# Decayed block attention followed by an ELU MLP: chunk 3 handled by head halves in separate PSUM banks, with the masks and the state work placed elsewhere

## The chip, the cores and the metric

The kernel runs on one core of one Trainium2 chip. The metric is the device time of one execution in microseconds (us), the median of several runs. A core has TensorE (PE in the profile; its weight loads are PEld), VectorE (DVE), ScalarE (ACT), GpSimd (POOL), and SyncE (SP), which here only issues transfers. Transfers issued by POOL go through one software queue (q0), those of SP and ACT through hardware queues; all share the core's 16 DMA engines.

## The reference

```python
# q, k, v: (4, 8, 768, 64) float32; lam: 8 decays near 0.98; w_in: 512 x 2048; w_out: 2048 x 512
block, nb = 64, S // 64
rel = pos[:, None] - pos[None, :]
Dmask = np.where(rel >= 0, lam[:, None, None] ** rel[None], 0.0)
lam_pow = lam[:, None, None] ** (pos[None, :, None] + 1)
lam_block = lam ** block
for b in range(nb):
    intra = np.einsum('bhic,bhjc->bhij', qb, kb) * Dmask[None]
    intra = np.einsum('bhij,bhjd->bhid', intra, vb)
    inter = np.einsum('bhid,bhde->bhie', qb * lam_pow[None], kv_state)
    out[:, :, sl] = intra + inter
    rev_pow = lam[:, None, None] ** (block - 1 - pos[None, :, None])
    kv_state = lam_block[None, :, None, None] * kv_state + np.einsum('bhsd,bhse->bhde', kb * rev_pow[None], vb)
# then, with x = out as (3072, 512):
h = x @ w_in
g = np.where(h > 0.0, h, np.exp(np.minimum(h, 0.0)) - 1.0)
return (g @ w_out).astype(np.float32)
```

## The kernel before, in words

The sequence is cut into blocks of L = 128 positions, not 64. A *chunk* g is one such block of one batch item: g = 4*(block) + (batch item), 24 chunks in all, so chunks 0 to 3 are the first block of the four items and have no incoming state. Four chunks make a token tile t of 512 rows, and there are six tiles. The input arrives as float32 and is cast to float16 by the transfer.

For a chunk, `att_T` transposes q and k on TensorE (L217) and `att_Te` copies the result out of PSUM to qT and kT (L229); `att_S` forms the scores (psS, L263); `att_mask` multiplies them by the decay mask on VectorE, giving P (L275); `att_O` multiplies P by v (L289) and, from the second block on, adds q times the state (L297); `att_X` writes the result to xt, the input of the MLP (L316, L318 for chunks 0 to 3, and L320 with the factor qs for later ones). `att_kd` scales k (L250), `att_U` forms the state's increment (psU, L337), `att_tmp` scales the old state on POOL (tmp, L354), and `att_st` makes the new state (L371 for the first block, a copy; L373 later, an addition). The state tiles `st` are zeroed first by memsets (L114), since only their diagonal head blocks are written. From chunk 10 on, q and k are transposed in pairs by transfers issued on SP (`att_xT`, L238).

For a tile, `mm1` computes one of 16 slices n of h (four matmuls into psH, L390), ScalarE makes e = exp(h) (L416) and r = relu(h) (L420), and VectorE combines them to g (L433). For three slices of tile 0 (`alt`) ScalarE makes e only, and VectorE does the rest in two operations (L428, L431). `mm2` adds slice n of one chunk to its output psM (L471); after n = 15 the output is copied (L485, L487) and stored (L488). The very last chunk is done by `mm2_last` in two halves of 256 columns (L446, L456, L458, L459).

The order is written by hand; each engine executes its instructions in program order. A head part treats chunks 0 to 3 one by one, with `warm(k)` fillers (matmuls on a constant, L497; their counts are the list W). Then come the steps A0 to A15 (mm1 of tile 0, from A10 on also mm2 of chunks 0 and 1), B0 to B15 (mm2 of chunks 2, 0 and 1), the steps (1, 0) to (5, 15), and E. At a step, mm1 comes first, then what `at` has put there, then the combination to g, then mm2. `visit(g, s0, s1, s2)` puts the parts of a pair of chunks at three steps: transposes and kd, scores and mask, output and state.

Inputs are loaded by POOL in the order of LOADS: q, k, v of chunks 0 to 3, w_in in seven pieces (wi), w_out in four (wo), and the later chunks in pairs. kd of chunks 0 and 2 stands in that list too and runs on POOL. LOADS 17 to 26 (up to the last wo) are issued before step A0, the rest at later steps.

PSUM has four kinds of buffers, each with two: S (two banks each), M and H (one bank each). A buffer is handed on when its readers have finished. The mask of the first block (`mask`, built for even and odd heads by `build_mask0`) is overwritten at A1 by `late_mask` with the mask of the later blocks.

Of the kernel before, what the change touches and what calls it, by code (L numbers as in the profile page):

```python
# [15 lines left out]
def kernel(  # L16
# [96 lines left out]
    def zero_state(j, i):  # L113
        nc.vector.memset(st[j][i][:], 0.0)  # L114

# [25 lines left out]
    lag = cpool.tile([128, 128], FP32, name="lag")  # L141
    nc.vector.tensor_copy(rel[:], rel_i[:])
    nc.vector.tensor_scalar_max(lag[:], rel[:], 0.0)
# [11 lines left out]
    )  # L155

# [11 lines left out]
    dn = cpool.tile([128, H], FP32, name="dn")  # L168
    nc.scalar.activation(dn[:], loglam[:], AF.Exp, scale=pos[:, 0:1])
# [5 lines left out]
    def late_mask():  # L175
        for hh in range(2):
            nc.vector.tensor_tensor(
                out=mask[:, hh],
                in0=causT[:].unsqueeze(1).broadcast_to([128, HP, 128]),
                in1=dn[:, hh::2].unsqueeze(2).broadcast_to([128, HP, 128]),  # L180
                op=ALU.mult,
            )

    def late_qs():
        nc.scalar.activation(ks[:], loglam[:], AF.Exp, scale=pos[:, 1:2])
        for hh in range(2):
            r = slice(hh * 64, (hh + 1) * 64)
            nc.scalar.copy(loglam_p[r, :], loglam[r, hh::2])
        nc.scalar.activation(up_p[:], loglam_p[:], AF.Exp, scale=float(L))
        for hp in range(HP):  # L190
            nc.scalar.activation(
                qs[:, hp, :], row[:], AF.Exp, scale=loglam_p[:, hp : hp + 1]
            )
# [28 lines left out]
    def att_Te(g, n, which, eng):  # L222
        j = "qk".index(which)
        pt = pT.pop((g, j))
        dst = asb.tile([128, n, HP, 128], FP16, tag=f"{which}T", name=f"{which}T{g}", bufs=3)
        if eng == "v":
            nc.vector.tensor_copy(dst[:], pt)
        else:
            nc.scalar.copy(out=dst[:], in_=pt)  # L229
        for i in range(n):  # L230
            (qT, kT)[j][g + i] = dst[:, i]

# [36 lines left out]
    def att_mask(g, parts=1):  # L269
        P = asb.tile([128, 2, HP, 128], FP16, tag="P", name=f"P{g}", bufs=3)  # L270
        s = pS.pop(g)
        w = HP // parts
        for i in range(parts):
            c = slice(i * w, (i + 1) * w)
            nc.vector.tensor_tensor(  # L275
                out=P[:, :, c], in0=s[:, :, c],
                in1=mask[:, :, c], op=ALU.mult,
            )
        Pt[g] = P
# [25 lines left out]
    def att_X(g, n, parts=1):  # L305
        t, i = where[g]
        if i == 0:
            xt[t] = asb.tile([128, HP, TS[t] * L], FP16, tag="xt", name=f"xt{t}")
        po = pS.pop(("O", g))
        w = HP // parts  # L310
        for j in range(parts):
            c = slice(j * w, (j + 1) * w)
            dst = xt[t][:, c, i * L : (i + n) * L].rearrange("p h (n l) -> p n h l", n=n)
            if g < B:
                if j == 1:
                    nc.vector.tensor_copy(dst, po[:, :, c])  # L316
                else:
                    nc.scalar.copy(out=dst, in_=po[:, :, c])  # L318
                continue
            nc.vector.tensor_tensor(  # L320
                out=dst, in0=po[:, :, c],
                in1=qs[:, c].unsqueeze(1).broadcast_to([128, n, w, 128]),
                op=ALU.mult,
            )
# [36 lines left out]
    def att_st(g):  # L361
        c, b = divmod(g, B)
        if c == NC - 1:
            return
        pu = pS.pop(("U", g))
        new = st[b // 2][(c + 1) % 2]
        for hh in range(2):
            r = slice(hh * 64, (hh + 1) * 64)
            if c == 0:
                copy = nc.scalar.copy if g in (0, 2) else nc.vector.tensor_copy  # L370
                copy(out=new[r, :, :, r], in_=pu[r])  # L371
            else:
                nc.vector.tensor_tensor(  # L373
                    out=new[r, :, :, r], in0=tmps[g][r], in1=pu[r], op=ALU.add
                )
        tmps.pop(g, None)
# [18 lines left out]
    def mm1(t, n, alt=False):  # L395
# [15 lines left out]
        else:  # L411
            if (t, n) not in pH_of:
                mm1_mm(t, n, 0, MT, "M" if t == 0 and n % 2 == 1 and n < 8 else "H")
# [23 lines left out]
    def mm2_last(t, i):  # L437
# [3 lines left out]
        hw = DM // 2  # L441
        for x in range(2):
            pm = ps.tile([128, hw], FP32, tag="M", bufs=2, name=f"psM{t}_{i}_{x}")
            cs = slice(x * hw, (x + 1) * hw)
            for n in range(NF):
                nc.tensor.matmul(  # L446
                    pm[:], lhsT=gt[t][:, n, i * L : (i + 1) * L],
                    rhs=wo_t[wo_at[n][0]][:, wo_at[n][1], cs],
                    start=(n == 0), stop=(n == NF - 1),
                )  # L450
            parts = 1 if x == 0 else 2
            w = hw // parts
            for y in range(parts):
                o = msb.tile([128, w], FP32, tag="osb", bufs=3, name=f"osl{x}{y}")
                if y == 0:
                    nc.vector.tensor_copy(o[:], pm[:, 0:w])  # L456
                else:
                    nc.scalar.copy(o[:], pm[:, w:])  # L458
                (nc.sync if y == 0 else nc.scalar).dma_start(  # L459
                    out=out[t0 : t0 + L, x * hw + y * w : x * hw + (y + 1) * w], in_=o[:]  # L460
                )
# [29 lines left out]
    def warm(k):  # L491
        if k <= 0:
            return
        pw = ps.tile([128, 4, 128], FP32, tag="M", bufs=2, name=f"psW{len(warms)}")
# [24 lines left out]
    W = [5, 2, 3, 0, 1, 0, 0, 0, 0, 0, 0]  # L519
# [7 lines left out]
    late_qs()  # L527
# [14 lines left out]
    zero_state(0, 1)  # L542
# [10 lines left out]
    att_O(1, 1, "M")  # L553
    warm(W[8])
    op_T(3, "k")
    op_Te(3, "k")
    att_X(1, 1)
# [4 lines left out]
    warm(W[9])  # L562
    for n in range(0):
        mm1_mm(0, n, 0, 3 * L, "HM"[n % 2])
    att_O(3, 1, "M")
    att_X(3, 1, 2)
    zero_state(1, 1)
    warm(W[10])
    for n in range(0, 1):
        mm1_mm(0, n, 0, 3 * L, "HM"[n % 2])  # L570
    for n in range(1):
        mm1_mm(0, n, 3 * L, 4 * L)

    at(('A', 1), late_mask)
    at(('A', 4), zero_state, 0, 0)
    at(('A', 4), zero_state, 1, 0)
    run_loads(LOADS[17:27])
    for s, g in zip([], (0, 2)):
        at(s, att_kd, g, 2)
    for s, g in zip([('A', 7), ('A', 9)], (0, 2)):  # L580
        at(s, att_U, g)
    for s, g in zip([('A', 8), ('A', 10)], (0, 2)):
        at(s, att_st, g)
        at(s, att_tmp, g + B)
# [25 lines left out]
    for g, vs in [(4, (('A', 12), ('A', 14), ('B', 1))), (6, (('B', 7), ('B', 10), ('B', 13))), (8, ((1, 0), (1, 2), (1, 5))), (10, ((1, 8), (1, 10), (1, 13))), (12, ((2, 0), (2, 2), (2, 5))), (14, ((2, 8), (2, 10), (2, 13))), (16, ((3, 0), (3, 2), (3, 5))), (18, ((3, 8), (3, 10), (3, 13))), (20, ((4, 0), (4, 2), (4, 5))), (22, ((4, 8), (4, 10), (4, 13)))]:  # L610
        visit(g, *vs)
    for s, a, b in [(('A', 14), 27, 28), (('A', 15), 28, 29), (('B', 11), 29, 30), (('B', 13), 30, 31), ((1, 1), 31, 32), ((1, 5), 32, 33), ((1, 9), 33, 34), ((1, 13), 34, 35)]:
# [3 lines left out]
    for s, m1, m2 in steps:  # L616
        er = None
        if m1 is not None:
            t, n = m1
            er = mm1(t, n, alt=t == 0 and n in (3, 5, 7))  # L620
# [36 lines left out]
```

## Time and profile before

| | us |
|---|---|
| median of 7 runs (lowest to highest) | 218.83 (218.29 to 220.65) |
| the profiled execution | 218.79 |
| its span, first to last instruction | 217.0 |
| PE busy in the span | 202.9 (94%) |
| DVE / ACT / POOL busy | 148.1 / 129.0 / 78.8 |
| PE busy in 40.00:45.00 | 3.57 of 5 |
| PE busy in 60.00:65.00 and in 75.00:90.00 | 5.00 of 5 and 15.00 of 15 |

The span is what the profile's views cover; 1.8 us lie around it. A busy PE only says that matmuls are in flight, so the place to look is where PE is idle and what ended that idle time. The mean granted TensorE clock is 1.000. A timeline row gives the start, the duration, the engine, the line, the operation, output<-input, the shape and the number of merged instructions; the brackets give the idle time before it on its engine and what ended it.

### The profile page before, as it was taken

How to read it: one execution, taken by the hardware profiler on the slowest of the kernel's cores; microseconds unless marked ns; L12 is line 12 of the kernel's file. 1: busy time of each engine (PE TensorE's matmuls, PEld its weight loads, DVE VectorE, ACT ScalarE, POOL GpSimd, SP SyncE). 2: the span in 40 equal slices, each digit the busy share in tenths (PEclk: the TensorE clock that was granted, in tenths of full speed). 3: DMA queues.
4: the chain of work that ended last, by engine and by line, in shares of the span. 5: the costliest groups of instructions: out<-in, count | busy, mean ns of one | idle time of the engine just before them, and what ended most of it. 6: DMA issues, size and time to landing. Idle time of an engine off the chain costs nothing.

```text
span 217.0 us, 3963 instructions
## 1 busy us (share of the span) xinstructions
PE 202.9 (94%) x1583; PEld 100.3 (46%) x1583; DVE 148.1 (68%) x190; ACT 129.0 (59%) x244; POOL 78.8 (36%) x76
## 2 busy tenths in 40 slices
PE   5867889799999999999999999999999999999992
PEld 1343335455554544544544545445445444444461
DVE  2466997978799999989886785775665544434010
ACT  6966799331978676466566466466556666674110
POOL 8999959998732947680400000000000000000000
PEclk9999999999999999999999999999999999999999
DMA  5999999999999999999952061061011011110221
GB/s 38 147 154 176 207 168 181 178 183 157 183 203 133 158 155 174 158 178 184 147 124 73 3 136 61 0 145 52 0 50 51 0 48 50 48 51 0 97 96 51
DMA packets 98899, 23.86 MB, mean 110 GB/s; under 512 B 90944, under 2 KB 95936, under 8 KB 98880
## 3 DMA queue, kind: packets, MB, share of 16 engines
q0 software_dynamic: 80208, 13.63, 82.3%
q1 hardware_dynamic: 18528, 9.90, 20.3%
q8 instruction: 12, 0.20, 0.4%
q10 hardware_dynamic: 144, 0.07, 0.1%
q14 instruction: 7, 0.06, 0.1%
HBM read 27.27 MB, written 6.29 MB: 155 GB/s over the span
## 4 chain that ended last, share of the span: by engine, by line
PE 68%; DMA 14%; POOL 8%; DVE 5%; ACT 2%; issue 1%; POOLq 0%; ACTq 0%
PE psM L471 32%; PE psH L390 28%; DMA kn<-in_k_dram 7%; DMA kT<-kn 5%; POOL tmp L354 3%; POOL qn L72 2%; DMA qn<-in_q_dram 2%; PE psS L263 2%; PE psO L289 2%; DVE g L433 2%; POOL kn L72 2%; PE psM L446 2%; PE psO L297 1%; POOL vn L72 1%; ACT r L420 1%
## 5 line engine op out<-in xcount | busy, mean ns | idle before, releaser
L390 PE MATMUL psH<-xt,wi 128*128 128x512 f16 (+2 forms) x388 | 97.7, 377 | 1.4 <-DVE g L431 0.7
L471 PE MATMUL psM<-wo,g 128*128 128x512 f16 x368 | 94.3, 380 | 0.6 <-DMA wo<-in_moe_w_out_dram 0.5
L433 DVE SCALAR_TENSOR_TENSOR g<-e,r 128x512 f16<-128x512 f32 x93 | 70.5, 776 | 35.5 <-ACT r L420 35.3
L416 ACT ACTIVATE e<-psH 128x512 f32<-128x512 f32 x96 | 57.5, 600 | 56.2 <-PE psH L390 52.6
L390 PEld LDWEIGHTS <-wi 128*128 128x128 f16 x388 | 37.5, 98 | 46.5 <-issue 2.5
L420 ACT ACTIVATE r<-psH 128x512 f16<-128x512 f32 x93 | 55.4, 596 | 0.0
L471 PEld LDWEIGHTS <-g 128*128 128x128 f16 x368 | 34.6, 98 | 41.0 <-DMA wo<-in_moe_w_out_dram 1.0
L275 DVE TENSOR_TENSOR P<-psS,mask 128x1024 f16<-128x1024 f32 (+1 forms) x28 | 28.7, 1066 | 5.1 <-PE psS L263 5.1
L354 POOL TENSOR_TENSOR tmp<-st,up_p 64x512 f32<-64x512 f16 x16 | 21.2, 1325 | 9.0 <-DVE st L373 7.9
L72 POOL DMA_DIRECT2D vn<-in_v_dram x14 | 15.1, 1088 | 8.1 <-issue 8.1
L72 POOL DMA_DIRECT2D kn<-in_k_dram x14 | 15.2, 1087 | 6.0 <-issue 5.9
L72 POOL DMA_DIRECT2D qn<-in_q_dram x14 | 15.7, 1119 | 3.4 <-issue 3.4
L320 DVE TENSOR_TENSOR xt<-psO,qs 128x1024 f16<-128x1024 f32 x10 | 12.2, 1220 | 5.6 <-PE psO L297 5.6
L487 ACT COPY osb<-psM 128x512 f32<-128x512 f32 x12 | 7.0, 591 | 15.2 <-PE psM L471 15.2
L289 PE MATMUL psO<-P,vn 128*64 128x128 f16 x192 | 12.5, 223 | 2.3 <-DVE P L275 2.3
L289 PEld LDWEIGHTS <-vn 128*64 128x64 f16 x192 | 10.0, 109 | 7.4 <-issue 6.6
L485 DVE COPY osb<-psM 128x512 f32<-128x512 f32 x11 | 7.6, 689 | 5.5 <-PE psM L471 5.4
L250 DVE TENSOR_TENSOR kd<-kn,ks 128x1024 f16<-128x1024 f16 x8 | 11.2, 1400 | 0.1
L373 DVE TENSOR_TENSOR st<-tmp,psU 64x512 f16<-64x512 f32 x16 | 10.9, 681 | 0.2
L297 PE MATMUL psO<-qT,st 128*64 128x128 f16 x160 | 10.2, 219 | 0.0
L263 PE MATMUL psS<-qT,kT 64*128 64x128 f16 x192 | 8.0, 221 | 1.2 <-ACT kT L229 0.8
L297 PEld LDWEIGHTS <-st 128*64 128x64 f16 x160 | 9.0, 110 | 0.0
(51 smaller groups left out, 87.4 us busy)
## 6 DMA issues: line engine op xcount, KB each, us to landing
out_dram<-osb SPq DMA_DIRECT2D x23, 256.0 KB, 2.0
qn<-in_q_dram POOLq DMA_DIRECT2D x10, 256.0 KB, 15.7
kn<-in_k_dram POOLq DMA_DIRECT2D x10, 256.0 KB, 16.2
vn<-in_v_dram POOLq DMA_DIRECT2D x10, 256.0 KB, 16.6
wo<-in_moe_w_out_dram POOLq DMA_DIRECT2D x4, 512.0 KB, 13.7
wi<-in_moe_w_in_dram POOLq DMA_DIRECT2D x2, 512.0 KB, 9.5
wi<-in_moe_w_in_dram POOLq DMA_DIRECT2D x3, 256.0 KB, 7.2
qn<-in_q_dram POOLq DMA_DIRECT2D x4, 128.0 KB, 4.8
```

Of the source, the lines that this page charges most:

```text
L72: nc.gpsimd.dma_start(out=dst, in_=src[b : b + n, :, rows].rearrange("b h p d -> p (b h) d"))
L263: nc.tensor.matmul(s[:, hh, hp, :], lhsT=kT[g][r, hp, :], rhs=qT[g][r, hp, :], start=True, stop=True,)
L275: nc.vector.tensor_tensor(out=P[:, :, c], in0=s[:, :, c], in1=mask[:, :, c], op=ALU.mult,)
L289: nc.tensor.matmul(po[r, i, hp, :], lhsT=v_of(g + i, 2 * hp + hh), rhs=P[:, hh, hp, :], start=True, stop=(c == 0), skip_group_check=True,)
L297: nc.tensor.matmul(po[r, i, hp, :], lhsT=st[(g + i) % B // 2][c % 2][:, (g + i) % 2, hp, r], rhs=qT[g + i][:, hp, :], start=False, stop=Tr ...
L320: nc.vector.tensor_tensor(out=dst, in0=po[:, :, c], in1=qs[:, c].unsqueeze(1).broadcast_to([128, n, w, 128]), op=ALU.mult,)
L354: e.tensor_tensor(out=tmp[r], in0=old[r, :, :, r], in1=up_p[r].unsqueeze(1).unsqueeze(3).broadcast_to([64, 2, HP, 64]), op=ALU.mult,)
L390: nc.tensor.matmul(pH[:, lo:hi], lhsT=wi[:, kk, j * 128 : (j + 1) * 128], rhs=xt[t][:, kk, lo:hi], start=(kk == 0), stop=(kk == HP - 1),)
L416: nc.scalar.activation(e[:], pH[:], AF.Exp)
L420: nc.scalar.activation(r[:], pH[:], AF.Relu)
L433: nc.vector.scalar_tensor_tensor(out=g, in0=e[:], scalar=-1.0, in1=r[:], op0=ALU.add, op1=ALU.min)
L471: nc.tensor.matmul(pm[:], lhsT=gt[t][:, n, i * L : (i + 1) * L], rhs=wo_t[wo_at[n][0]][:, wo_at[n][1], :], start=(n == 0), stop=(n == NF - 1),
```

## The change

- The states' four memsets and both masks are made near the start, before `build_mask0`; the mask of the later blocks has a tile of its own, `mask1`. `lag` now shares the tile of `rel`.
- `late_qs` is split: ks, loglam_p and up_p stay (`late_up`), and the four rows of qs follow in two pairs, behind X(2) and behind the first mm1.
- X(0) is copied by VectorE. X(1) comes before the transposes of k(3).
- k(3)'s transposes and its copies (`att_T2`), and O(3) with X(3) (`att_OX2`), go by halves of the heads, each half in an H bank of its own; ScalarE copies the first half and VectorE the second.
- W has three more fillers: one each at W[5], W[8] and W[9].
- The slices of tile 0 below n = 8 use M for even n and H for odd n (it was the other way round), and `alt` applies to n = 2, 4, 6 instead of 3, 5, 7.
- `att_U` of chunks 0 and 2 moves from A7 and A9 to A5 and A7; `att_st` and `att_tmp` of them from A8 and A10 to A6 and A8. The state copy of chunk pair 0 goes to VectorE.
- The last two wo loads (LOADS 25 and 26) move from before A0 to A9 and A10.
- The third step of `visit(4)` (output and state) moves from B1 to B2.
- The last chunk is done in pieces of 256, 128 and 128 columns, in banks M, M and H, copied by VectorE, ScalarE and VectorE and stored from SP, ACT and SP.

```diff
     ]
-    def zero_state(j, i):
-        nc.vector.memset(st[j][i][:], 0.0)
-
...
     def run_loads(items):
...
     rel = cpool.tile([128, 128], FP32, name="rel")
-    lag = cpool.tile([128, 128], FP32, name="lag")
     nc.vector.tensor_copy(rel[:], rel_i[:])
-    nc.vector.tensor_scalar_max(lag[:], rel[:], 0.0)
     nc.vector.tensor_scalar(
...
     )
+    lag = rel
+    nc.vector.tensor_scalar_max(lag[:], rel[:], 0.0)
+    for j in range(B // 2):
+        for i in range(2):
+            nc.vector.memset(st[j][i][:], 0.0)
+    dn = cpool.tile([128, H], FP32, name="dn")
+    nc.scalar.activation(dn[:], loglam[:], AF.Exp, scale=pos[:, 0:1])
+    mask1 = cpool.tile([128, 2, HP, 128], FP32, name="mask1")
+    for hh in range(2):
+        nc.vector.tensor_tensor(
+            out=mask1[:, hh],
+            in0=causT[:].unsqueeze(1).broadcast_to([128, HP, 128]),
+            in1=dn[:, hh::2].unsqueeze(2).broadcast_to([128, HP, 128]),
+            op=ALU.mult,
+        )
     def build_mask0(hh):
...
     build_mask0(0)
-    dn = cpool.tile([128, H], FP32, name="dn")
-    nc.scalar.activation(dn[:], loglam[:], AF.Exp, scale=pos[:, 0:1])
     ks = cpool.tile([128, H], FP32, name="ks")
...
     loglam_p = cpool.tile([128, HP], FP32, name="loglam_p")
-    def late_mask():
-        for hh in range(2):
-            nc.vector.tensor_tensor(
-                out=mask[:, hh],
-                in0=causT[:].unsqueeze(1).broadcast_to([128, HP, 128]),
-                in1=dn[:, hh::2].unsqueeze(2).broadcast_to([128, HP, 128]),
-                op=ALU.mult,
-            )
-
-    def late_qs():
+    def late_up():
         nc.scalar.activation(ks[:], loglam[:], AF.Exp, scale=pos[:, 1:2])
...
         nc.scalar.activation(up_p[:], loglam_p[:], AF.Exp, scale=float(L))
-        for hp in range(HP):
+    def late_qs(lo, hi):
+        for hp in range(lo, hi):
             nc.scalar.activation(
...
             (qT, kT)[j][g + i] = dst[:, i]
+    def att_T2(g, which, tag):
+        j = "qk".index(which)
+        nat = heads((qn, kn)[j], g)
+        dst = asb.tile([128, 1, HP, 128], FP16, tag=f"{which}T", name=f"{which}T{g}", bufs=3)
+        w = HP // 2
+        for x in range(2):
+            t1 = ps.tile([128, w, 128], FP16, tag=tag, bufs=2, name=f"psT{which}{g}_{x}")
+            for y in range(w):
+                hp = x * w + y
+                nc.tensor.transpose(
+                    t1[:, y, :], in_=nat[:, 2 * hp : 2 * hp + 2, :], identity=ident16[:]
+                )
+            copy = nc.vector.tensor_copy if x else nc.scalar.copy
+            copy(out=dst[:, 0, x * w : (x + 1) * w], in_=t1[:])
+        (qT, kT)[j][g] = dst[:, 0]
+    def att_OX2(g, tag):
+        t, i = where[g]
+        P = Pt.pop(g)
+        w = HP // 2
+        for x in range(2):
+            po = ps.tile([128, w, 128], FP32, tag=tag, bufs=2, name=f"psO{g}_{x}")
+            for y in range(w):
+                hp = x * w + y
+                for hh in range(2):
+                    r = slice(hh * 64, (hh + 1) * 64)
+                    nc.tensor.matmul(
+                        po[r, y, :], lhsT=v_of(g, 2 * hp + hh), rhs=P[:, hh, hp, :],
+                        start=True, stop=True, skip_group_check=True,
+                    )
+            copy = nc.vector.tensor_copy if x else nc.scalar.copy
+            copy(out=xt[t][:, x * w : (x + 1) * w, i * L : (i + 1) * L], in_=po[:])
     def att_xT(g):
...
                 out=P[:, :, c], in0=s[:, :, c],
-                in1=mask[:, :, c], op=ALU.mult,
+                in1=(mask if g < B else mask1)[:, :, c], op=ALU.mult,
             )
...
             if g < B:
-                if j == 1:
-                    nc.vector.tensor_copy(dst, po[:, :, c])
-                else:
-                    nc.scalar.copy(out=dst, in_=po[:, :, c])
+                copy = nc.vector.tensor_copy if g == 0 else nc.scalar.copy
+                copy(out=dst, in_=po[:, :, c])
                 continue
...
             if c == 0:
-                copy = nc.scalar.copy if g in (0, 2) else nc.vector.tensor_copy
+                copy = nc.scalar.copy if g in (2,) else nc.vector.tensor_copy
                 copy(out=new[r, :, :, r], in_=pu[r])
...
             if (t, n) not in pH_of:
-                mm1_mm(t, n, 0, MT, "M" if t == 0 and n % 2 == 1 and n < 8 else "H")
+                mm1_mm(t, n, 0, MT, "M" if t == 0 and n % 2 == 0 and n < 8 else "H")
             pH = pH_of.pop((t, n))
...
         t0 = b * S + c * L
-        hw = DM // 2
-        for x in range(2):
-            pm = ps.tile([128, hw], FP32, tag="M", bufs=2, name=f"psM{t}_{i}_{x}")
-            cs = slice(x * hw, (x + 1) * hw)
+        x0 = 0
+        for x, (w, tag) in enumerate([(256, 'M'), (128, 'M'), (128, 'H')]):
+            pm = ps.tile([128, w], FP32, tag=tag, bufs=2, name=f"psM{t}_{i}_{x}")
             for n in range(NF):
...
                     pm[:], lhsT=gt[t][:, n, i * L : (i + 1) * L],
-                    rhs=wo_t[wo_at[n][0]][:, wo_at[n][1], cs],
+                    rhs=wo_t[wo_at[n][0]][:, wo_at[n][1], x0 : x0 + w],
                     start=(n == 0), stop=(n == NF - 1),
                 )
-            parts = 1 if x == 0 else 2
-            w = hw // parts
-            for y in range(parts):
-                o = msb.tile([128, w], FP32, tag="osb", bufs=3, name=f"osl{x}{y}")
-                if y == 0:
-                    nc.vector.tensor_copy(o[:], pm[:, 0:w])
-                else:
-                    nc.scalar.copy(o[:], pm[:, w:])
-                (nc.sync if y == 0 else nc.scalar).dma_start(
-                    out=out[t0 : t0 + L, x * hw + y * w : x * hw + (y + 1) * w], in_=o[:]
-                )
+            o = msb.tile([128, w], FP32, tag="osb", bufs=3, name=f"osl{x}")
+            (nc.scalar.copy if x % 2 else nc.vector.tensor_copy)(o[:], pm[:])
+            (nc.scalar if x % 2 else nc.sync).dma_start(
+                out=out[t0 : t0 + L, x0 : x0 + w], in_=o[:]
+            )
+            x0 += w
     def mm2(t, i, n, tag="M"):
...
         psM.pop((t, i))
-    def warm(k):
+    def warm(k, tag="M"):
         if k <= 0:
             return
-        pw = ps.tile([128, 4, 128], FP32, tag="M", bufs=2, name=f"psW{len(warms)}")
+        pw = ps.tile([128, 4, 128], FP32, tag=tag, bufs=2, name=f"psW{len(warms)}")
         warms.append(pw)
...
     def op_Te(c, w):
         att_Te(c, 1, w, "a")
-    W = [5, 2, 3, 0, 1, 0, 0, 0, 0, 0, 0]
+    W = [5, 2, 3, 0, 1, 1, 0, 0, 1, 1, 0]
     warm(W[0])
...
     op_Te(0, "k")
-    late_qs()
+    late_up()
     warm(W[2])
...
     att_mask(1, 2)
-    zero_state(0, 1)
     op_T(2, "q")
...
     att_O(1, 1, "M")
+    att_X(1, 1)
     warm(W[8])
-    op_T(3, "k")
-    op_Te(3, "k")
-    att_X(1, 1)
+    att_T2(3, "k", "H")
+    warm(W[9])
     att_S(3)
...
     att_X(2, 1)
-    warm(W[9])
+    late_qs(0, 2)
+    warm(W[10])
     for n in range(0):
-        mm1_mm(0, n, 0, 3 * L, "HM"[n % 2])
-    att_O(3, 1, "M")
-    att_X(3, 1, 2)
-    zero_state(1, 1)
-    warm(W[10])
+        mm1_mm(0, n, 0, 3 * L, "MH"[n % 2])
+    att_OX2(3, "H")
     for n in range(0, 1):
-        mm1_mm(0, n, 0, 3 * L, "HM"[n % 2])
+        mm1_mm(0, n, 0, 3 * L, "MH"[n % 2])
+    late_qs(2, HP)
     for n in range(1):
         mm1_mm(0, n, 3 * L, 4 * L)
-    at(('A', 1), late_mask)
-    at(('A', 4), zero_state, 0, 0)
-    at(('A', 4), zero_state, 1, 0)
-    run_loads(LOADS[17:27])
+    run_loads(LOADS[17:25])
     for s, g in zip([], (0, 2)):
         at(s, att_kd, g, 2)
-    for s, g in zip([('A', 7), ('A', 9)], (0, 2)):
+    for s, g in zip([('A', 5), ('A', 7)], (0, 2)):
         at(s, att_U, g)
-    for s, g in zip([('A', 8), ('A', 10)], (0, 2)):
+    for s, g in zip([('A', 6), ('A', 8)], (0, 2)):
         at(s, att_st, g)
...
             t, n = m1
-            er = mm1(t, n, alt=t == 0 and n in (3, 5, 7))
+            er = mm1(t, n, alt=t == 0 and n in (2, 4, 6))
         do(s)
```

More of the change, by code (lines that the diff above doesn't have):

```diff
@@ L608, in visit @@
         at(s2, att_tmp, g + B)
-    for g, vs in [(4, (('A', 12), ('A', 14), ('B', 1))), (6, (('B', 7), ('B', 10), ('B', 13))), (8, ((1, 0), (1, 2), (1, 5))), (10, ((1, 8), (1, 10), (1, 13))), (12, ((2, 0), (2, 2), (2, 5))), (14, ((2, 8), (2, 10), (2, 13))), (16, ((3, 0), (3, 2), (3, 5))), (18, ((3, 8), (3, 10), (3, 13))), (20, ((4, 0), (4, 2), (4, 5))), (22, ((4, 8), (4, 10), (4, 13)))]:
+    for g, vs in [(4, (('A', 12), ('A', 14), ('B', 2))), (6, (('B', 7), ('B', 10), ('B', 13))), (8, ((1, 0), (1, 2), (1, 5))), (10, ((1, 8), (1, 10), (1, 13))), (12, ((2, 0), (2, 2), (2, 5))), (14, ((2, 8), (2, 10), (2, 13))), (16, ((3, 0), (3, 2), (3, 5))), (18, ((3, 8), (3, 10), (3, 13))), (20, ((4, 0), (4, 2), (4, 5))), (22, ((4, 8), (4, 10), (4, 13)))]:
         visit(g, *vs)
-    for s, a, b in [(('A', 14), 27, 28), (('A', 15), 28, 29), (('B', 11), 29, 30), (('B', 13), 30, 31), ((1, 1), 31, 32), ((1, 5), 32, 33), ((1, 9), 33, 34), ((1, 13), 34, 35)]:
+    for s, a, b in [(('A', 9), 25, 26), (('A', 10), 26, 27), (('A', 14), 27, 28), (('A', 15), 28, 29), (('B', 11), 29, 30), (('B', 13), 30, 31), ((1, 1), 31, 32), ((1, 5), 32, 33), ((1, 9), 33, 34), ((1, 13), 34, 35)]:
         at(s, run_loads, LOADS[a:b])
```

## The prediction

> **What bounds the kernel now.** I read the page's slices first. TensorE is full from about 49 us on and its granted clock is full throughout, so time can only come out of the first third, or of the last microseconds. The DMA row shows the second resource: it is saturated from slice 2 to about 60 us.
>
> ```profile
> PE   5867889799999999999999999999999999999992
> PEclk9999999999999999999999999999999999999999
> DMA  5999999999999999999952061061011011110221
> ```
>
> Next the timeline of TensorE up to 72 us, looking for waits on transfers. The brackets give the idle time before the row and what ended it.
>
> ```profile
> 20.11 4.49 PE L390 MATMUL psH<-xt,wi 128*128 128x512 f16 x20 [0.48 <-DMA wi<-in_moe_w_in_dram]
> 30.43 0.60 PE L471 MATMUL psM<-wo,g 128*128 128x512 f16 x2 [0.49 <-DMA wo<-in_moe_w_out_dram]
> 34.15 0.62 PE L217 MATMUL psT<-ident,kn 128*128 128x128 f16 x8 [0.29 <-DMA kn<-in_k_dram]
> ...
> 38.00 0.59 PE L471 MATMUL psM<-wo,g 128*128 128x512 f16 x2
> 39.77 2.34 DVE L275 TENSOR_TENSOR P<-psS,mask 128x1024 f16<-128x1024 f32 x2
> 41.03 0.25 PE L289 MATMUL psO<-P,vn 128*64 128x128 f16 x2 [0.94 <-DVE P L275]
> 42.17 0.25 PE L289 MATMUL psO<-P,vn 128*64 128x128 f16 x2 [0.49 <-DVE P L275]
> 45.62 2.11 PE L471 MATMUL psM<-wo,g 128*128 128x512 f16 x9
> 47.80 0.45 PEld L263 LDWEIGHTS <-kT 64*128 64x128 f16 x16 [0.57 <-ACT kT L229]
> ...
> 69.05 0.62 PE L263 MATMUL psS<-qT,kT 64*128 64x128 f16 x16 [0.26 <-DMA kT<-kn]
> ```
>
> TensorE meets a landing at 20.1, 30.4, 34.15 and 69.05. Between them it waits for VectorE (P) and ScalarE (kT). The POOL timeline and the issue table, cut to one issue each (the last number is us to landing), give the other landings:
>
> ```profile
> wo<-in_moe_w_out_dram POOLq DMA_DIRECT2D x1, 512.0 KB, 12.6
> wo<-in_moe_w_out_dram POOLq DMA_DIRECT2D x1, 512.0 KB, 14.8
> wo<-in_moe_w_out_dram POOLq DMA_DIRECT2D x1, 512.0 KB, 15.4
> ```
>
> ```profile
> 30.69 0.75 POOL L104 DMA_DIRECT2D wo<-in_moe_w_out_dram  x1 [1.12 <-DMA wo<-in_moe_w_out_dram]
> 32.60 0.74 POOL L104 DMA_DIRECT2D wo<-in_moe_w_out_dram  x1 [1.16 <-DMA qn<-in_q_dram]
> 33.36 5.94 POOL L354 TENSOR_TENSOR tmp<-st,up_p 64x512 f32<-64x512 f16 x4
> 39.24 1.22 POOL L72 DMA_DIRECT2D qn<-in_q_dram  x1
> ```
>
> wo chunk 1 (issued at 25.33) lands at 37.9, exactly where step A14 needs it (38.00). Chunk 2 lands at 30.69+14.8 = 45.5, and step B8 first uses it: the row of nine at 45.62 is B7 to B9, so B8 starts at 45.62+3x0.216 = 46.27. Chunk 3 lands at 48.0 and is used near 49.7. Transfers and TensorE thus run almost level up to 69 us, and that caps what this change can bring. Last, the end:
>
> ```profile
> 212.91 0.29 DVE L456 COPY osl<-psM 128x128 f32<-128x128 f32 x1 [1.27 <-PE psM L446]
> 213.28 0.27 ACT L458 COPY osl<-psM 128x128 f32<-128x128 f32 x1 [3.28 <-DVE osl L456]
> 213.58 0.37 ACTq L459 DMA_DIRECT2D out_dram<-osl  x1
> ```
>
> ScalarE waits for VectorE although it reads other columns: two readers of one bank run one after the other.
>
> **The change, part by part.**
>
> *Up to 20.1 us: nothing.* k(3) is now copied in halves. ScalarE does X(1) first (0.59, from O(1)'s end at 14.5), then its half (0.37, the 128x256 CAST row) to about 15.4. VectorE's half stands behind P(2), which ends at 15.48, and takes 0.42 (its 128x256 row) to 15.9; before, kT(3) was ready at 15.45. S(3) and, queued behind it, O(2) and O(3) wait for that; P(3) starts near 16.25 instead of 15.94 and ends at 17.55. What is lost returns in X(3): its halves no longer follow one another (17.62 to 18.45 before), and VectorE's ends near 17.9+0.42 = 18.35. The first mm1 is complete at about 18.75, as before, and the second about 0.15 later, against 0.48 of wait for wi at 20.11. The three extra fillers (14 for 11, 0.216 each, 0.65 in all) lie in gaps for landings at 12.5 and 13.4 and for kT and P; without that cover they cost 0.65. late_qs (1.26 of ScalarE) leaves 9.05 to 10.31, where it delayed qT(1) by 0.2, but q/k landings hold the transposes at 12.5 and 13.4 anyway.
>
> *VectorE's new work at 2.6 to 6.5 us: 0.1 late.* Four memsets (0.48 each) and two mask1 products (0.68) make 3.28 us, in a stretch in which VectorE idled 3.70; build_mask0(0) slips from 6.15 to 6.5 and P(0) at 9.5 does not notice. But POOL is issuing loads there. The rows: a wi issue under a memset (18.43) took 0.81, the wo issues 0.74 to 0.81; under build_mask0's product an issue took 0.91 to 0.93 against 0.88. That is 0 to 0.05 per operation, at most 0.3 for six; I take 0.1. The Trainium skill, page SBUF — State Buffer, section "SBUF: two separate sides", speaks against it: VectorE operations that use the port pair shared with GpSimd keep GpSimd from writing descriptors until they end. By it all 3.28 could be added to every later landing, since the saturated queue never wins time back. I stay with the rows and keep 3.28 as the far end.
>
> *20 to 30 us: much freed, nothing gained.* late_mask (1.20) and the memsets (0.48+0.48) stood in the chain that ran through VectorE from 19.9 to 28.3 and held TensorE 0.65 at 25.25; two state copies (1.17) leave ScalarE for VectorE (2x0.69). Steps A0 to A9 are ten mm1 of 0.864 and two att_U of 0.4: from 20.1 and n=2 on, 8x0.864+0.8 = 7.7, so n=9 ends near 27.9 and n=10 near 29.1 with ScalarE's pace of 0.97 a step. Then wo chunk 0 is late next: 30.4, as before.
>
> *30 to 47 us: up to 0.97.* k(4) at 34.1 and wo chunk 1 at 37.95 hold TensorE to its old times, so A14's mm2 is at 38.0. What changes is VectorE after that. The four tmp (5.94) move ahead of the two last wo issues on POOL, to about 29.6–35.5 (from the end of v(6)'s issue). Beside them VectorE is slow: kd 2.06 at 34.90 against 1.23 at 45.79, g 1.52 and 1.53 at 36.88 against 0.69. In the new place VectorE has slack, kd(4) ends near 36 and P(4), P(5) near 39.2 and 40.4 (S(4) at 37.9 gates them), not 40.95 and 42.1. O(4) is one mm2 step later in the order: 38.0+0.43+0.86+0.43+2x0.216 = 40.2, and finds P ready. B8 could then start at 44.5 and waits for wo chunk 2: 45.53+0.1. S(6) follows six mm2 later at 46.9 instead of 47.80, kT(6) being ready by 46. That is 0.97-0.1 = 0.87. The two wo issues slip to about 35.5–37; the queue is then filled to 42.95 (v(6)'s landing), so their landings do not move. tmp(6) now waits for ScalarE's state copy near 29.3; behind it on POOL wait those wo issues and loads (8..10). If the cover went (issue later than about 40.5), each us would cost one.
>
> *47 to 69 us: 0.05 to 0.1 lost.* The three stores at 54.00 come 0.87 earlier. They and qT stand ahead of kT(10) in SP's queue, so kT(10) (58.73, 10.3 to landing) should come earlier by nearly as much; but they also take transfer time from k(10), which starts it. Between 0 and 0.87 of the gain survives; I take 0.8, since qT occupies the queue while k(10) lands. After 69 us TensorE never idles; kT(12) lands at 78.8, used near 80.
>
> *The end: 0.3.* 16 matmuls of 256 (3.51/32 = 0.110) and 32 of 128. The rows for 128 columns with fresh weights start 0.055 to 0.056 apart (transposes at 45.17, 0.45 for eight). So 1.76+1.79 = 3.55, 0.04 more. The last VectorE copy ends near 213.25 and SP issues at 213.27, not 213.58. The skill's page TensorE: Matmul & The Clock Gate, section "Back-to-back issue gap", says about 81 ns per matmul in a stream of weight loads at 128 columns: 32x0.025 = 0.8 more, and the tail would lose 0.5. The row decides.
>
> Sum: -0.8-0.3 = -1.1 on the profiled execution, 218.79 (span 217.0 and 1.8 around it); the median of the runs is 218.83, so 217.7.
>
> **Rivals.** 0.5%, 1.1 us, is about what a measurement of this kernel can tell from no change.
>
> A (0.47): as above, somewhat to its good side, 217.2 to 217.74; the 0.26 wait at 69.05 may go too.
>
> B (0.39): the middle is lost again. kT(10) is tied to k(10), which lands at the same time or later, or P(5) still comes after 41.5; TensorE waits at 69 instead. Left are the tail's 0.3, or nothing: 217.75 to 218.9, typically 218.5. For it: three landings in a row already pin TensorE, and 0.26 of wait stands there. Against it: kT(10) landed 10.3 after its issue, behind the stores.
>
> C (0.14): slower. The early VectorE operations hold POOL's descriptors by s; all landings and B8 move by s. The gain is 0.97+0.3-s, a loss of over 1.1 from s = 2.4, and at s = 3.28 it is +2.0: 220.8. For it: the first q issue took 1.06 beside four VectorE operations, later ones 0.88. Against it: the rows above.
>
> That the halves do not separate the engines would cost only the 0.3 of slack in the head.
>
> **How the numbers follow.** The likeliest gives 217.7. The range reaches from 217.0 (A with the wait at 69 gone, -1.5, and 0.3 of scatter) to 219.2 (all of B), leaving out C and a little of A. Faster 0.47, same 0.39, slower 0.14.
>
> **What would show it.** The wo wait at 30.4 grows to about 1.3; no wait for P near 41 to 42; instead one of up to 1 us for wo near 45.5; tmp near 30–35; S(6) near 46.9; S(10) near 68.2; last issue on SP, 0.3 after the last matmul. Wrong if early loads land more than 0.3 later, if wo chunk 2 lands after 46.5, or if S(10) is still at 69.

## The result, and the profile after

The changed kernel takes 217.41 us (median of 12 runs, 216.92 to 218.5) against 218.92 (31 runs) of the kernel before beside it: the ratio is 0.9936, with a 95% interval of 0.992 to 0.9952. Its profiled execution has a span of 215.7 us, 1.3 shorter than before; the traces can explain these 1.3, not the 1.5 between the medians. The ratios here and below are of fast executions alone, while the medians take in all (two experiments had one slow execution near 268 us each), so a ratio is not the quotient of two medians.

The slices of the page (5.4 us each) show the same picture as before: the DMA row stands at 9 up to slice 20, about 108 us, and TensorE is full from slice 10, about 49 us, on.

```profile
PE   4878979989999999999999999999999999999993
PEclk9999999999999999999999999999999999999999
DMA  5999999999999999999961061061011011110222
```

The timeline of TensorE and VectorE between 28 and 48 us shows where the middle part of the gain is, and what limits it.

```profile
30.60 0.60 PE L499 MATMUL psM<-wo,g 128*128 128x512 f16 x2 [1.07 <-DMA wo<-in_moe_w_out_dram]
...
38.17 0.59 PE L499 MATMUL psM<-wo,g 128*128 128x512 f16 x2 [0.34 <-DMA wo<-in_moe_w_out_dram]
38.34 2.34 DVE L311 TENSOR_TENSOR P<-psS,mask 128x1024 f16<-128x1024 f32 x2
...
45.74 1.46 PE L499 MATMUL psM<-wo,g 128*128 128x512 f16 x6 [0.83 <-DMA wo<-in_moe_w_out_dram]
47.12 0.45 PEld L299 LDWEIGHTS <-kT 64*128 64x128 f16 x16 [0.42 <-issue]
```

The wait for wo chunk 0 has grown from 0.49 to 1.07: what VectorE and ScalarE were relieved of before 30 us brings nothing there. P(4) and P(5) start at 38.34 instead of 39.77, and the two waits for them (0.94 and 0.49) are gone. The wait at 45.74 is new; it ends with wo chunk 2. S(6) starts at 47.12, 0.68 earlier.

The reason for the earlier P stands in the rows of POOL and VectorE:

```profile
29.35 6.72 DVE L467 SCALAR_TENSOR_TENSOR g<-e,r 128x512 f16<-128x512 f32 x5
29.76 5.77 POOL L388 TENSOR_TENSOR tmp<-st,up_p 64x512 f32<-64x512 f16 x4
...
36.00 1.21 DVE L286 TENSOR_TENSOR kd<-kn,ks 128x1024 f16<-128x1024 f16 x1
37.13 1.28 DVE L467 SCALAR_TENSOR_TENSOR g<-e,r 128x512 f16<-128x512 f32 x2
```

Before, with tmp at 33.36 to 39.30, the same kd and two g were these:

```profile
34.90 2.06 DVE L250 TENSOR_TENSOR kd<-kn,ks 128x1024 f16<-128x1024 f16 x1
36.88 2.97 DVE L433 SCALAR_TENSOR_TENSOR g<-e,r 128x512 f16<-128x512 f32 x2
```

tmp now runs at 29.8 to 35.5. It still slows what stands beside it: four of the five g there took 1.5 us each. But kd (1.21, not 2.06) and the next two g (1.28 for both, not 2.97) are clear of it. Taken singly, the rows look as if the two engines took turns: each of the four slow g ends 0.54 to 0.55 us after a tmp has ended, and before, the tmp that started while kd was under way took 1.90 and ended 0.90 after kd, where a tmp with VectorE idle for most of its time took 1.05.

At 69.05 TensorE used to wait 0.26 for the transfer that transposes k(10). The scores of chunk 10 now start at 68.06 without a wait, 0.99 earlier, and this 0.99 is carried unchanged to the last scores (their start is 159.06 against 160.05). SP's queue shows when that transfer went out, after:

```profile
53.33 1.37 SPq L516 DMA_DIRECT2D out_dram<-osb  x3
55.56 1.48 SPq L274 DMA_TRANSPOSE qT<-qn  x1
57.28 3.99 SPq L274 DMA_TRANSPOSE kT<-kn  x1
```

and before, where the stores began at 54.00:

```profile
57.01 1.47 SPq L238 DMA_TRANSPOSE qT<-qn  x1
58.73 3.72 SPq L238 DMA_TRANSPOSE kT<-kn  x1
```

kT(10) goes out when k(10) has landed: k(10) was issued at 41.77 and landed at 57.27, and before it was issued at 43.87 and landed at 58.72. So kT(10) started 1.45 earlier because its input came 1.45 earlier, while the stores ahead of it in the queue moved by 0.67 only.

And the end, where each copy now has its own bank:

```profile
210.68 1.99 SPq L486 DMA_DIRECT2D out_dram<-osl  x2
211.06 0.27 ACT L485 COPY osl<-psM 128x128 f32<-128x128 f32 x1 [2.05 <-PE psM L479]
211.36 0.37 ACTq L486 DMA_DIRECT2D out_dram<-osl  x1
212.01 0.29 DVE L485 COPY osl<-psM 128x128 f32<-128x128 f32 x1 [1.36 <-PE psM L479]
```

ScalarE's copy waits for TensorE alone. From the first matmul of the last chunk to the end of the span it takes 215.69-208.22 = 7.47 us, and it was 216.99-209.22 = 7.77. So 1.0 comes from the middle and 0.3 from the end, which is the span's 1.3.

### The profile page after: what moved, and what is told of

It is laid out like the page before. It is cut to its first block, busy times and chain, and to the rows that moved or that the text cites. A ratio compares the mean times of both kernels' runs of the same rounds, so it can differ in the third digit from the quotient of the medians.

```text
span 215.7 us, 4003 instructions
## 1 busy us (share of the span) xinstructions
PE 203.4 (94%) x1602; PEld 100.7 (47%) x1602; DVE 151.1 (70%) x194; ACT 127.6 (59%) x241; POOL 79.1 (37%) x76
## 4 chain that ended last, share of the span: by engine, by line
PE 76%; POOL 10%; DMA 9%; ACT 2%; issue 1%; DVE 0%; POOLq 0%; DVEq 0%
PE psM L499 35%; PE psH L424 32%; DMA wo<-in_moe_w_out_dram 9%; POOL wi L97 2%; PE psO L325 2%; PE psS L299 2%; PE psO L333 2%; POOL kd L286 2%; POOL qn L72 2%; PE psM L479 2%; POOL kn L72 2%; POOL vn L72 2%; POOL tmp L388 1%; PE psU L371 1%; ACT e L450 1%
## 5 line engine op out<-in xcount | busy, mean ns | idle before, releaser
L467 DVE SCALAR_TENSOR_TENSOR g<-e,r 128x512 f16<-128x512 f32 x93 | 71.8, 792 | 34.4 <-ACT r L454 34.2
L325 PE MATMUL psO<-P,vn 128*64 128x128 f16 x184 | 11.7, 222 | 0.1
L325 PEld LDWEIGHTS <-vn 128*64 128x64 f16 x184 | 9.5, 109 | 4.7 <-issue 4.0
L286 DVE TENSOR_TENSOR kd<-kn,ks 128x1024 f16<-128x1024 f16 x8 | 9.9, 1243 | 0.1
```

Source lines behind the costliest of these rows:

```text
L286: e.tensor_tensor(out=kd[:].rearrange("p (n h) d -> p n h d", n=n), in0=heads(kn, g, n).rearrange("p (n h) d -> p n h d", n=n), in1=ks_b, ...
L325: nc.tensor.matmul(po[r, i, hp, :], lhsT=v_of(g + i, 2 * hp + hh), rhs=P[:, hh, hp, :], start=True, stop=(c == 0), skip_group_check=True,)
L467: nc.vector.scalar_tensor_tensor(out=g, in0=e[:], scalar=-1.0, in1=r[:], op0=ALU.add, op1=ALU.min)
```

## The experiments

My theory was: the state scaling moved out of the way of VectorE makes the middle gain, transfers limit it, the end makes the rest, and everything done to the head is idle time exchanged for idle time. The rivals were that the masks and memsets made early free VectorE, or that the halves of chunk 3 do it. Medians below are given against the kernel before in the same set of runs, since sets on different chips are not to be subtracted.

### The state work alone

```diff
-    run_loads(LOADS[17:27])
+    run_loads(LOADS[17:25])
-    for s, g in zip([('A', 7), ('A', 9)], (0, 2)):
+    for s, g in zip([('A', 5), ('A', 7)], (0, 2)):
         at(s, att_U, g)
-    for s, g in zip([('A', 8), ('A', 10)], (0, 2)):
+    for s, g in zip([('A', 6), ('A', 8)], (0, 2)):
...
-    for s, a, b in [(('A', 14), 27, 28), ...
+    for s, a, b in [(('A', 9), 25, 26), (('A', 10), 26, 27), (('A', 14), 27, 28), ...
```

> The kernel before, with one part of the change: the state products, state copies and tmp of chunks 0 to 3 two steps sooner, and the last two wo loads behind tmp on POOL. Theory (tmp out of VectorE's way): P(5) ends before 41 instead of at 42.1, TensorE then waits for wo chunk 2 near 45.6, and the run is 0.5 to 0.8 us faster than before. Rival (the early masks and memsets free VectorE, and that makes the gain): within 0.2 us of before. Rival (the head halves make it): within 0.2 us of before.

Measured: 218.28 against 218.93, ratio 0.9969 (0.9942 to 0.9996). P(5) ended at 41.12 (expected: before 41), S(6) began at 46.81, 1.0 earlier than before. The wait for wo chunk 2 that was expected near 45.6 was only about 0.1, since the chunk landed at 45.37. But most of the 1.0 was taken back at the scores of chunk 10:

```profile
68.75 0.62 PE L263 MATMUL psS<-qT,kT 64*128 64x128 f16 x16 [0.94 <-DMA kT<-kn]
```

So up to S(6) this one part makes the middle gain by itself, without the early masks and without the halves. At S(10) only 0.3 of it is left in this profile, because the transfer kT(10) is a second limit.

### The head halves undone

```diff
-                copy = nc.vector.tensor_copy if g == 0 else nc.scalar.copy
+                copy = nc.vector.tensor_copy if g == 0 or j == 1 else nc.scalar.copy
...
-    W = [5, 2, 3, 0, 1, 1, 0, 0, 1, 1, 0]
+    W = [5, 2, 3, 0, 1, 0, 0, 0, 0, 0, 0]
...
-    att_X(1, 1)
     warm(W[8])
-    att_T2(3, "k", "H")
+    op_T(3, "k")
+    op_Te(3, "k")
+    att_X(1, 1)
...
-    att_OX2(3, "H")
+    att_O(3, 1, "M")
+    att_X(3, 1, 2)
```

> The changed kernel with chunk 3 of the head done whole again: its k transposes and copy on one bank and one engine, O(3) and X(3) as before, X(1) behind kT(3), and without the three extra fillers. Theory (the wi landing at 19.4 to 20.1 and the wo landing at 30.5 swallow the head): within 0.2 us of the changed kernel, about 1.4 us faster than the kernel before. Rival (the halves carry part of the gain): 0.4 us or more slower than the changed kernel.

> The changed kernel with chunk 3 of the head done whole again and without the extra fillers, once more. Theory: 1.3 to 1.6 us faster than before, as the changed kernel. Rival (halves carry part): 1.0 us or less faster.

Measured: ratios 0.9936 (0.9917 to 0.9956) and, in the second set, 0.9937 (0.9912 to 0.9962), against 0.9936 of the changed kernel. The halves and the fillers together are worth no time that these runs can measure (they do show in the granted clock; see the last section). The rows of the halves in the changed kernel's head, in the timeline, say why:

```profile
15.31 0.38 ACT L248 COPY kT<-psTk 128x256 f16<-128x256 f16 x1
15.69 0.28 DVE L248 COPY kT<-psTk 128x256 f16<-128x256 f16 x1
15.74 0.57 PE L299 MATMUL psS<-qT,kT 64*128 64x128 f16 x8 [0.20 <-ACT kT L248]
16.36 1.29 DVE L311 TENSOR_TENSOR P<-psS,mask 128x512 f16<-128x512 f32 x2 [0.39 <-PE psS L299]
```

Each half copy is short, but they end one after the other, since VectorE is busy with P(2) up to 15.8. P(3) starts at 16.36; before it was 15.94. Whatever the head wins or loses, TensorE then meets wo chunk 0: in the two profiles without the halves it waits 0.64 and 0.85 for it and starts at 30.14 and 30.34, in the changed kernel 1.07 and 30.60.

### The old end on the changed kernel, and the new end on the kernel before

The first restores the two pieces of 256 columns, with VectorE and ScalarE sharing the bank of the second; the other puts the new loop into the kernel before.

```diff
-        x0 = 0
-        for x, (w, tag) in enumerate([(256, 'M'), (128, 'M'), (128, 'H')]):
+        hw = DM // 2
+        for x in range(2):
...
```

> The changed kernel with the last chunk in two halves of 256 columns again. Theory (two readers of one bank run one after the other at the end): 0.3 to 0.4 us slower than the changed kernel, the last store issue again 0.6 us after the last matmul's end instead of 0.3. Rival (128-column matmuls cost 81 ns each and eat the gain): the same as the changed kernel or faster by up to 0.5 us.

> The kernel before with only the last chunk in pieces of 256, 128 and 128 columns. Theory (the end is worth 0.35 by itself): from the start of the last matmul to the end of the span 4.0 us instead of 4.4, the last matmul 0.04 later, the median 0.3 to 0.4 us faster than before. Rival (128-column matmuls at 81 ns): the last matmul 0.8 later and the run 0.4 us slower.

Measured: ratio 0.9935 (0.9913 to 0.9958) with the old end on the changed kernel, and 0.9994 (0.9972 to 1.0015) with the new end on the kernel before. The medians resolve neither: 0.3 us is 0.0014, and the intervals are three times as wide. The old end on the changed kernel was not slower by the 0.3 to 0.4 that was expected (217.54, beside 217.49 for the kernel without halves in the same set); the new end on the kernel before was faster by 0.31, as expected, with an interval that includes no change. The traces do resolve it. From the start of the last matmul to the end of the span it takes 4.38 to 4.39 us in the three profiles with the old end (before, the state work alone, the old end put back), and 3.99 to 4.00 in all ten with the new one. The last chunk's matmuls take 3.48 us from first to last start instead of 3.38. The net is 0.3, whichever kernel it is in. At 81 ns for each 128-column matmul, the rival's figure, that stretch would have been about 4.3 us (an estimate: 31 starts, each 0.025 later).

### The state work put back late

```diff
-    run_loads(LOADS[17:25])
+    run_loads(LOADS[17:27])
-    for s, g in zip([('A', 5), ('A', 7)], (0, 2)):
+    for s, g in zip([('A', 7), ('A', 9)], (0, 2)):
         at(s, att_U, g)
-    for s, g in zip([('A', 6), ('A', 8)], (0, 2)):
+    for s, g in zip([('A', 8), ('A', 10)], (0, 2)):
...
```

> The changed kernel with the state work of chunks 0 to 3 back at its old steps (A7 to A10) and the last two wo loads ahead of tmp on POOL again. Theory (tmp beside VectorE's kd and g of 35 to 40 us delays P): tmp runs near 33 to 39, kd and two g take 2.0 and 1.5 each again, P(5) ends near 41.7 instead of 40.7, O(4) and O(5) wait, S(6) starts 0.3 to 0.8 later, and the run is 0.3 to 0.8 us slower than the changed kernel. Rival (the masks and memsets made early are what frees VectorE): within 0.2 us of the changed kernel.

The changed kernel stood in the same set:

> The changed kernel itself, beside the others on one chip: 1.3 to 1.6 us faster than before, the wait for wo chunk 2 near 45.5 there again, about 1 us.

Measured: 218.35, ratio 0.996 (0.9937 to 0.9984), with the state work late; 217.42, ratio 0.9931 (0.9908 to 0.9955), for the changed kernel, whose expected wait for wo chunk 2 did not come (see below). The medians differ by 0.93, a little more than the 0.3 to 0.8 of the theory, the ratios by 0.0029 or 0.6 us, and the two intervals overlap. The timeline of the first shows the mechanism:

```profile
34.18 5.94 POOL L388 TENSOR_TENSOR tmp<-st,up_p 64x512 f32<-64x512 f16 x4
...
35.72 2.06 DVE L286 TENSOR_TENSOR kd<-kn,ks 128x1024 f16<-128x1024 f16 x1
...
37.70 2.97 DVE L467 SCALAR_TENSOR_TENSOR g<-e,r 128x512 f16<-128x512 f32 x2
...
41.98 0.25 PE L325 MATMUL psO<-P,vn 128*64 128x128 f16 x2 [0.84 <-DVE P L311]
...
43.11 0.25 PE L325 MATMUL psO<-P,vn 128*64 128x128 f16 x2 [0.49 <-DVE P L311]
```

With both masks still made early, kd takes 2.06 and the two g 2.97 again, to the hundredth what they took before, and both waits for P are back. This is against the rival of the masks as the cause in the middle. S(6) started at 48.52, but loads landed about 0.6 late in this profile (wo chunk 1 at 38.77), so its absolute times are not to be compared. In the medians this kernel is still 0.6 faster than the one before, of which the end accounts for 0.3; whether the rest is scatter or other parts of the change, the interval does not tell.

### Two parts together

The kernel before with the state work of the first experiment and the new end of the third.

> The kernel before with two parts of the change: the state work sooner with the last two wo loads behind tmp, and the new end. Theory (these two make the gain): 1.0 to 1.5 us faster than before, within 0.3 us of the kernel without the head halves beside it. Rival (the masks and memsets made early, and the copies shifted between ScalarE and VectorE, carry the rest): 0.5 us or more slower than the kernel without the head halves.

Measured: 217.91, ratio 0.9941 (0.992 to 0.9962), beside 217.54 and 0.9937 for the changed kernel without halves. The difference of 0.4 in the medians (0.1 by the ratios) lies between what the theory and the rival expected, and within the scatter. The two parts carry at least most of the gain; that the other parts add 0.1 to 0.4 is not excluded. The early masks and memsets, the shifted copies, the exchange of M and H and the third step of `visit(4)` at B2 were never run by themselves. One place where they might count: the two kernels that have the state work without them waited 0.94 and 0.87 for kT(10), the eight profiles of the changed kernel and its near relatives (all but the late state work) 0 to 0.65. Landings scatter by more than that, so this stays open.

### Taking the next limit away

```diff
-    ... ('wo', 1), (6, 2), ('wo', 2), ('wo', 3), (8, 2), ...
+    ... ('wo', 1), (6, 2, 'qk'), ('wo', 2), ('wo', 3), (6, 2, 'v'), (8, 2), ...
```

> The changed kernel with one load moved: v of chunks 6 and 7 behind the last two pieces of wo. Theory (the landing of wo chunk 2 at 45.7 is what bounds the changed kernel in the middle): chunk 2 lands near 43.5 and chunk 3 near 46, the wait of 1.0 near 45.7 goes, v lands near 48.2 before O(6) needs it at 48.8, and the run is 0.7 to 1.0 us faster than the changed kernel. Rival (something later, the transposes by transfer for chunk 10 near 68, bounds it anyway): the wait moves to about 67 to 68 and the run is within 0.2 us of the changed kernel.

> The changed kernel with v of chunks 6 and 7 behind the last two pieces of wo, once more, beside the changed kernel. Theory (with the wait for wo chunk 2 gone, the wait for P(5) near 41 and then for kT(6) is next): 0.2 to 0.5 us faster than the changed kernel. Rival (its gain in the first run came from that run's earlier landings): within 0.1 us of the changed kernel.

Measured: ratio 0.992 (0.9898 to 0.9942) in the first set, 217.21; in the second 217.26 beside 217.42 for the changed kernel, ratio 0.9924 (0.9907 to 0.9941) against 0.9931. It was not slower in either set, but 0.16 us in the same set is less than the runs resolve. The first expectation (0.7 to 1.0) missed, and the second (0.2 to 0.5) was not reached. The edit did its part: chunk 2 landed at 43.6, and the wait for it is gone in the timeline. Two others have come forward.

```profile
41.11 0.25 PE L325 MATMUL psO<-P,vn 128*64 128x128 f16 x2 [0.49 <-DVE P L311]
...
44.35 2.11 PE L499 MATMUL psM<-wo,g 128*128 128x512 f16 x9
46.52 0.45 PEld L299 LDWEIGHTS <-kT 64*128 64x128 f16 x16 [0.57 <-ACT kT L230]
```

P(5) at 41.06 instead of 40.68, and kT(6) behind it, hold S(6) at 46.5. P(5) in turn was late because VectorE, just before P(4), stood idle for ScalarE's r (1.08 here; 0.23 to 1.09 in the profiles with P(5) at 41.1, none in those with 40.5 to 40.7). The changed kernel's own second profile shows the same limits, because its wo chunk 2 happened to land at 44.6; there 0.65 was lost again at kT(10):

```profile
41.16 0.25 PE L325 MATMUL psO<-P,vn 128*64 128x128 f16 x2 [0.49 <-DVE P L311]
...
46.58 0.45 PEld L299 LDWEIGHTS <-kT 64*128 64x128 f16 x16 [0.57 <-ACT kT L230]
...
68.23 0.62 PE L299 MATMUL psS<-qT,kT 64*128 64x128 f16 x16 [0.65 <-DMA kT<-kn]
```

So wo chunk 2, P(5) with kT(6), and kT(10) lie within about 1 us of each other. Taking wo chunk 2 away uncovered the others.

### The early memsets doubled

```diff
             nc.vector.memset(st[j][i][:], 0.0)
+            nc.vector.memset(st[j][i][:], 0.0)
```

> The changed kernel with each of the four early memsets done twice, 2 us more of VectorE beside POOL's first load issues. Theory (the operations near 3 to 7 us do not hold POOL's descriptors up): POOL's issue times are the same to 0.05, and q, k, v and wi land within the scatter of the other profiles, wo chunk 2 between 44.6 and 46.4. Rival (VectorE locks POOL out): the issues after 3 us or the landings are 1 to 2 us later.

Measured in a single execution: 217.15 us. POOL's load issues beside the memsets, in the timeline:

```profile
3.29 0.88 POOL L72 DMA_DIRECT2D vn<-in_v_dram  x1
3.43 0.48 DVE L156 MEMSET st<- 128x512 uint32 x1 [0.17 <-DVE st L155]
...
4.16 0.89 POOL L72 DMA_DIRECT2D qn<-in_q_dram  x1
4.62 0.48 DVE L156 MEMSET st<- 128x512 uint32 x1 [0.17 <-DVE st L155]
```

The issues stand within 0.03 of the kernel before, which has no memset there, and q, k, v landed within 0.2 of it, some earlier and some later. wo chunk 2 landed at 44.5, the earliest of the profiles with this order of loads. These memsets do not hold POOL's issue of transfers up. Nor do the two mask1 products, at 5.18 to 6.47 in the changed kernel: its issues up to 11.09 stand within 0.01 of those before. The rival fell, and so did my 0.1.

## Why the prediction was right, point by point

- *Median.* 217.7 forecast, 217.41 measured. Of the profiled execution's 1.3, 1.1 was forecast. That it came so close is in part luck: the gain at S(6) was 0.19 smaller than forecast, and between 47 and 69 us, where a loss was forecast, 0.31 was won.
- *What bounds the kernel.* One reading was wrong: the DMA row stands at 9 up to about 108 us, not 60. It did not matter, since TensorE waits for no transfer after 69 us in either profile.
- *Up to 20 us: nothing.* Right: the halves undone change nothing. ScalarE's half copy took 0.38 (0.37 forecast), VectorE's 0.28 (0.42), and P(3) started at 16.36 (16.25).
- *20 to 30 us: much freed, nothing gained.* Right: the wait for wo chunk 0 grew, to 1.23 us if it is counted from when the next matmul could have been issued (1.3 forecast).
- *30 to 47 us: 0.87.* The mechanism was right: tmp at 29.8 to 35.5 (29.6 to 35.5), P(5) at 40.68 (40.4), S(6) at 47.12 (46.9), so 0.68. B8 waited 1.0 for wo chunk 2 (0.83 as idle time in the row above, the rest the tail of the matmul before), as forecast. What I had not foreseen is that P(5) ends at 41.1 in five of eight profiles of the changed kernel and its near relatives (40.5 to 40.7 in the other three), behind a wait for ScalarE, and is then a limit of its own.
- *The early VectorE work: 0.1 late.* Here the term was mis-sized: nothing was measured. In this profile q, k and v landed up to 0.33 later, which touches the prediction's own sign of being wrong (0.3), and wo 0.17 later. But it is scatter: v(2), the latest of them, landed at 15.47 here and at 14.66 to 15.46 in the other profiles with the early VectorE work, at 14.99 to 15.29 in those without it. The rows of the trace were the better guide for these operations, and still too high. The lock of which the prediction cites the rule did not show; since no run tells whether a memset or a mask product takes the shared ports, the rule itself was not tested.
- *47 to 69 us: 0.05 to 0.1 lost.* Wrong in sign, and in what was thought to set it: 0.68 at S(6) became 0.99 at S(10), as the wait of 0.26 also went. The stores did go out earlier (53.33 instead of 54.00), but what released kT(10) was the landing of k(10), 1.45 earlier, after an issue 2.1 earlier on POOL. The prediction knew that k(10) starts kT(10) and expected the stores to take transfer time from it; case B had it land at the same time or later. It does not hold in each run: over all the profiles k(10) landed between 56.45 and 58.72, and in three with the early state work TensorE waited 0.65, 0.87 and 0.94 for kT(10), in two more 0.20 and 0.24. Case B's limit is thus real, but takes a part, not all.
- *The end: 0.3.* Right, 0.30 from the traces. The 128-column rate from the rows (0.056) held; the 81 ns of the Trainium skill's page TensorE: Matmul & The Clock Gate, section "Back-to-back issue gap", do not apply to these matmuls.

## What to carry to other kernels

When transfers and the bounding engine run nearly level, write down the landing of each load beside the time of its first use; the smallest difference caps the gain of any change upstream of it, however much work that change frees. GpSimd elementwise work is not free because GpSimd is idle: place it where VectorE has slack, since here VectorE's SBUF operations beside it took about twice as long (g 1.52 for 0.68, kd 2.06 for 1.21). And a saving of 0.1% is read from the trace, not from a median.

## What the runs showed of the hardware that I had not expected

TensorE's clock fell to half in two profiles: with the new end on the kernel before from 15.3 to 22.2 us, and with the state work and the new end from 17.8 to 21.2. The page of the first:

```profile
PEclk9995999999999999999999999999999999999999
```

No idle stretch of TensorE was longer than about 1 us there, but it was busy for only 2.40 of 4 us at 10 to 14. Both kernels have the head of the kernel before, with 11 fillers.

The mean granted clock is known for every execution of the experiments and of the changed kernel, not only for the profiled ones. A mean below 0.995 stands for more than about 2.2 us at half clock (an estimate: half of 2.2 us, over a span of 217). Of 46 executions of kernels with the halves and the three extra fillers, none was below 0.996 (the one near 268 us is left aside). Of the 22 of the changed kernel without both, 14 were below 0.995, though the early masks are in it; of 66 of the kernel before in the three sets of the experiments (one of 224 us left aside), 31. So the early masks do not keep the clock up. Something of what was undone together does (the halves, the fillers, the place of X(1)); which of it stays open. TensorE's busy time from 14 to 18 us goes with it: 3.06 of 4 us in all seven profiles with these parts, 2.58 or 2.59 in five of the six without (the sixth, with 2.94, was at half clock by then).

A dip is not always free. In the kernel before, the median of the executions below 0.995 stood above that of the others by 0.8 us in one set, 0.4 in another and -0.1 in the third. In the two profiles with a dip the first product with wo chunk 0 started at 30.92 and 30.77 without waiting for the chunk (landed at 30.60 and 30.04), so the dip had used up the slack there and more. This may be why the medians differ by more than the profiled executions, whose clocks were 1.000 and 0.999; that is not shown, since the changed kernel without halves and fillers was as fast in its medians.

The landings of one and the same queue of loads, issued at the same times up to 28 us, drift by up to 1.9 us from run to run by 45 us (wo chunk 2: 44.5 to 46.4, in the profiles with the same order of loads). This is larger than the gain studied here.
